# Two token columns to a list product: one-hots of 64 places, two of four blocks of the result in use

## The chip, the cores and the metric

One Trainium2 chip, one of its cores. The metric is the device time of one execution in microseconds (us). Engines are named as in the profile: PE is TensorE's matmul stream, PEld its weight loads, DVE is VectorE, ACT is ScalarE, POOL is GpSimd, SP is SyncE.

## The reference

A 2-D Fourier transform of `x`, a mixture of experts with a capacity for each expert, and a two-layer feed-forward network with a leaky activation:

```python
X = np.fft.fft(np.fft.fft(x, axis=1), axis=2).real          # x: 8 x 3072 x 256
x = X.reshape(24576, 256)

logits = x @ w_gate                                          # 8 experts
order = np.argsort(-logits.flatten())                        # best scores first
# each token goes to the first expert of this order that has room (cap = 3072 tokens)
for e in range(8):
    out[mask[e]] = np.maximum(x[mask[e]] @ w1[e], 0) @ w2[e]

h = out @ w_in
g = np.maximum(h, 0) + alpha * np.minimum(h, 0)
return g @ w_out
```

## The kernel before

It has two stages. The first (0 to about 370 us) does the Fourier transform and writes the tokens to DRAM, with their logits kept on the chip. The second (`ffn_phase`, the rest) fills the experts one after another, in eight rounds: a round finds the next expert to be full and its 3072 tokens, and the feed-forward network then runs over them in 6 tiles of 512 tokens, 48 tiles in all.

The network's products are split into high and low float32 parts, three matmuls for each. In the code of a tile (`for i in range(8)`) stand the layers `l1` (tile `h`), two of `l3` (tile `u`), `l2` (`y`) and two of `l4` (`o`), of the present and the previous tile: six steps to an `i`, each of 6 matmuls of 512 columns or 12 of 256. After a step's matmuls are written, one piece of the routing of the *next* expert is put in by `next(bg, None)`, and then the evacuation of that layer by ACT and DVE. The program is written out in this order and no scheduler moves it (`manual_schedule`): each engine works through its own instructions in the order in which they stand. `router.beat` counts the steps, and `yield from self.lag()` lets two of them go by, so that what DVE has just been given can be ready before TensorE comes to the matmul that reads it.

The last part of a round (`place`, then `pack`) makes the expert's token list. `si` is each token's place in the list (0 to 3071; others lie outside it). Tokens lie as 128 partitions x 192 columns. A place is split into a low part, `lh[:, 0]` (7 bits, 128 values), and a high part, `lh[:, 1]` (24 values in use). For each column of 128 tokens, a one-hot of the low part (`ol`, 128 wide) is the stationary operand, and a one-hot of the high part, multiplied once by the partition number (`self.pf`) and once by the column number (`self.colb`), is the moving operand (`rr`, 2 x 24 = 48 wide). The sum over all 192 columns, in the tile `ls`, is the list: for each place its token's partition and column. `pack` makes the one-hots for 8 columns at a time (a chunk: `eq`, `ol`, and two `rr` on DVE, lines 650 to 653), and after two chunks and a lag it issues their 16 matmuls (line 659). That is 12 groups of 16 to a list. The first list is made by another function (`pack_wide`); the other seven by `pack`, beside the network's matmuls. The list is then copied (`lm`), turned into row numbers (`idx`), and read by `gather_x`, which fetches the tokens of a tile by indirect DMAs from POOL's queue.

What loads the weights: each matmul reads one column of a chunk, `ol[:, :, j]`, that is 128 values that lie 8 elements apart.

Of the kernel before, what the change touches and what calls it, by code (L numbers as in the profile page):

```python
# [10 lines left out]
F32 = mybir.dt.float32  # L11
F32R = mybir.dt.float32r
BF16 = mybir.dt.bfloat16
I32 = mybir.dt.int32
I16 = mybir.dt.int16
# [3 lines left out]
ALU = mybir.AluOpType  # L19
# [4 lines left out]
P = 128  # L24
B, N, D = 8, 3072, 256
E = 8
TOK = B * N
N1, N2 = 96, 32
NG = 24
HC = 138  # L30
CV = 256
NCOL = TOK // P
# [236 lines left out]
class Router:  # L269
# [20 lines left out]
    def __init__(self, ctx, tc, LG):  # L290
        nc = self.nc = tc.nc
        self.LG = LG
        rp = ctx.enter_context(tc.tile_pool(name="r_state", bufs=1))
        V = nc.vector
        self.oh = rp.tile([P, NCOL, E], BF16, name="oh")
        self.aw = rp.tile([P, NCOL], BF16, name="aw")
        self.hi = rp.tile([P, NCOL], F32, name="hi")
        self.lo = rp.tile([P, NCOL], F32, name="lo")
        self.k16 = rp.tile([P, NCOL], I16, name="k16")
        self.done = rp.tile([P, NCOL], BF16, name="done")  # L300
        self.base = rp.tile([P, 1], F32, name="base")
        self.hstar = rp.tile([P, 1], F32, name="hstar")
        self.ohe = self.oh.rearrange("p a e -> p (a e)").rearrange("p (e a) -> p e a", e=E)
        self.eid = rp.tile([P, E], F32, name="eid")
        self.wm = rp.tile([P, 1], F32, name="wm")
        self.estar = rp.tile([P, 1], F32, name="estar")
        V.memset(self.done, 0.0)

        self.wE = rp.tile([P, E], BF16, name="wE")
        self.colb = rp.tile([P, NCOL], BF16, name="colb")  # L310
        self.mskj = rp.tile([P, 16], F32, name="mskj")
        self.mske = rp.tile([P, E], F32, name="mske")
        self.ones = rp.tile([P, P], F16, name="ones")
        self.onesb = rp.tile([P, NCOL], BF16, name="onesb")
        self.tri = rp.tile([P, P], BF16, name="tri")
        self.triA = rp.tile([96, NCOL], BF16, name="triA")
        self.triB = rp.tile([96, NCOL], BF16, name="triB")
        self.pf = rp.tile([P, 1], F32, name="pf")
        with tc.tile_pool(name="r_init", bufs=1) as ip:
            ci = ip.tile([P, NCOL], I32, name="ci")  # L320
            nc.gpsimd.iota(ci, pattern=[[1, NCOL]], base=0, channel_multiplier=0)
            cf = ip.tile([P, NCOL], F32, name="cf")
            V.tensor_copy(cf, ci)
            pi = ip.tile([P, 3], I32, name="pi")
            nc.gpsimd.iota(pi, pattern=[[0, 3]], base=0, channel_multiplier=1)
            V.tensor_copy(self.pf, pi[:, :1])
            V.tensor_scalar(self.wE, cf[:, :E], -1.0, float(E), op0=ALU.mult, op1=ALU.add)
            V.tensor_copy(self.colb, cf)
            V.tensor_copy(self.eid, cf[:, :E])
            V.tensor_scalar(pi[:, 1:2], pi[:, 0:1], 3, None, op0=ALU.logical_shift_right)  # L330
            V.tensor_scalar(pi[:, 2:3], pi[:, 0:1], 7, None, op0=ALU.bitwise_and)
            pq = ip.tile([P, 3], F32, name="pq")
            V.tensor_copy(pq, pi)
            V.tensor_scalar(self.mskj, cf[:, :16], pq[:, 1:2], None, op0=ALU.is_equal)
            V.tensor_scalar(self.mske, cf[:, :E], pq[:, 2:3], None, op0=ALU.is_equal)
            V.memset(self.ones, 1.0)
            V.memset(self.onesb, 1.0)

            V.tensor_scalar(self.tri, cf[:, :P], self.pf, None, op0=ALU.is_gt)
            V.tensor_scalar(self.triA, cf[:96], self.pf[:96], None, op0=ALU.is_gt)  # L340
            V.tensor_scalar(self.triB, cf[:96], self.pf[:96], 96.0, op0=ALU.subtract, op1=ALU.is_gt)

    def open_work(self, ctx, tc):
        self.wp = wp = ctx.enter_context(tc.tile_pool(name="r_work", bufs=1))
        self.ilo = wp.tile([P, P, self.CH], I16, name="ilo")
        self.ihi = wp.tile([P, self.CH, NG], I16, name="ihi")

    def prep(self, wp, view, n):
# [50 lines left out]
    def count_wide(self, psum, pool, key, lows, k, at0=None):  # L399
# [18 lines left out]
        for h, H in ((0, 10), (10, 10), (20, 4)):  # L418
            sh = [P, H, k - first, 8]
            V.tensor_tensor(  # L420
                ind[:, h : h + H, first:k], blocks(key)[:, h : h + H, None, :].broadcast_to(sh),
                lows[:, None, 16 - k + first :, :].broadcast_to(sh), op=ALU.is_ge,
            )
            for c in range(h, h + H):
                nc.tensor.matmul(
                    dv, ind[:, c, :k].rearrange("p k j -> p (k j)"), self.oh[:, 8 * c : 8 * c + 8],
                    start=(c == 0), stop=(c == NG - 1),
                )
# [15 lines left out]
    def first(self, psum, lists, pool):  # L444

        nc, wp = self.nc, self.wp
        V = nc.vector
# [6 lines left out]
            nc.gpsimd.iota(lows[step], pattern=[[step, 16], [0, 8]], base=-32768, channel_multiplier=0)  # L454
        ilo = pool.tile([P, P, 16], I16, name="ilo")
        nc.gpsimd.iota(ilo, pattern=[[1, P], [0, 16]], base=0, channel_multiplier=0)
        nc.gpsimd.iota(self.ilo, pattern=[[1, P], [0, self.CH]], base=0, channel_multiplier=0)
        nc.gpsimd.iota(self.ihi, pattern=[[0, self.CH], [1, NG]], base=0, channel_multiplier=0)
        yield "start"
        self.warm(24)  # L460
# [71 lines left out]
    def place(self, psum, lists, at, n, wide=None, ilo=None):  # L532


        nc, wp = self.nc, self.wp
        V = nc.vector
# [36 lines left out]
        si = wp.tile([P, NCOL], I16, tag="si", name="si")  # L573
        V.scalar_tensor_tensor(si, s12[:, 0], 30000.0, s12[:, 1], op0=ALU.add, op1=ALU.add)
        lh = wp.tile([P, 2, NCOL], I16, tag="lh", name="lh")
        V.tensor_scalar(lh[:, 0], si, 127, None, op0=ALU.bitwise_and)
        V.tensor_scalar(lh[:, 1], si, 7, None, op0=ALU.logical_shift_right)
        yield
        ls = psum(name="ls")
        lv = ls[:, : 2 * NG].rearrange("p (a g) -> p a g", a=2)  # L580
        lm, idx = lists
        yield from (self.pack_wide(wide, lv, lh, ilo) if wide else self.pack(lv, lh))
        V.tensor_copy(lm, lv)
        V.scalar_tensor_tensor(idx, lm[:, 1], float(P), lm[:, 0], op0=ALU.mult, op1=ALU.add)
        yield "list"
        if n == 1:
            return

        V.scalar_tensor_tensor(self.done, lh[:, 1], float(NG), self.done, op0=ALU.is_lt, op1=ALU.max)
        pen = wp.tile([P, 2, E - 1], F32, tag="pen", name="pen")  # L590
        for i, op in enumerate((ALU.is_le, ALU.is_gt)):
            V.tensor_scalar(pen[:, i, : n - 1], self.wE[:, : n - 1], self.wm, -BIG, op0=op, op1=ALU.mult)
# [2 lines left out]
        for c in range(-1, NCOL // H):  # L595
            g = self.LG[:, c * H : c * H + H] if c >= 0 else self.eid[:, None, :]
# [10 lines left out]
    def pack_wide(self, pool, lv, lh, ilo):  # L607

        nc, V = self.nc, self.nc.vector
        C = 16  # L610
        self.warm(14)
# [3 lines left out]
        H = NCOL // 4  # L615
        for c in range(0, NCOL, C):
            if c % H == 0:
# [10 lines left out]
                )  # L628
            ol = pool.tile([P, P, C], BF16, tag="ol", bufs=2, name="ol")
            V.tensor_tensor(ol, lh[:, 0, None, c : c + C].broadcast_to([P, P, C]), ilo, op=ALU.is_equal)  # L630
            for j in range(C):
                nc.tensor.matmul(
                    lv, ol[:, :, j], rr[:, c + j], start=(c + j == 0), stop=(c + j == NCOL - 1)
                )
            self.warm(2 if c % H == H - C else 1)
            yield

    def pack(self, lv, lh):

        nc, wp, V = self.nc, self.wp, self.nc.vector  # L640
        C = self.CH
        for c2 in range(0, NCOL // C, 2):
            made = []
            for c in (c2, c2 + 1):
                s = slice(c * C, c * C + C)
                ol = wp.tile([P, P, C], BF16, tag="ol", bufs=2, name="ol")

                eq = wp.tile([P, C, NG], BF16, tag="eq", bufs=2, name="eq")
                rr = wp.tile([P, C, 2, NG], BF16, tag="rr", bufs=2, name="rr")
                V.tensor_tensor(eq, lh[:, 1, s, None].broadcast_to([P, C, NG]), self.ihi, op=ALU.is_equal)  # L650
                V.tensor_tensor(ol, lh[:, 0, None, s].broadcast_to([P, P, C]), self.ilo, op=ALU.is_equal)
                V.tensor_scalar(rr[:, :, 0], eq, self.pf, None, op0=ALU.mult)
                V.tensor_tensor(rr[:, :, 1], eq, self.colb[:, s, None].broadcast_to([P, C, NG]), op=ALU.mult)
                made.append((c, ol, rr))
                yield
            yield from self.lag()
            for c, ol, rr in made:
                for j in range(C):
                    nc.tensor.matmul(  # L659
                        lv, ol[:, :, j], rr[:, j], start=(c == 0 and j == 0),  # L660
                        stop=(c == NCOL // C - 1 and j == C - 1),
                    )
            yield

    def rank(self, n):

# [691 lines left out]
```

## Time and profile before

| | |
|---|---|
| median of 3 runs | 3851.39 us (3847.69 to 3852.5) |
| profiled execution, its own time | 3852.32 us |
| its span, first to last instruction | 3850.2 us |
| granted TensorE clock, mean over the span | 0.994 of full |
| PE busy, share of the span | 3781.4 us, 98% |
| DVE busy | 2523.0 us, 66% |
| ACT busy | 1817.5 us, 47% |
| POOL busy | 566.2 us, 15% |

A share of busy time is an average over both stages. The ends of matmuls are modelled, and matmuls overlap, so what a matmul costs is read from the distance between starts, and not from its duration.

### The profile page before, as it was taken

What the parts mean: (1) busy time and instruction counts of PE and PEld (TensorE: products, weight loads), DVE (VectorE), ACT (ScalarE), POOL (GpSimd) and SP (SyncE); (2) the same over time, 40 slices, a digit from 0 to 9 for tenths busy, and PEclk for the clock granted to TensorE, in tenths of its full rate; (3) what the DMA queues carried; (4) which work ended last, traced back from release to release, by engine and by line L of the source; (5) the groups of instructions that cost most, each with busy time, mean ns of one, the idle gap of its engine ahead of it and who ended that gap; (6) DMA issues with size and microseconds to landing.
All of it is one profiled execution on the core that took longest, in us unless ns stands there. A gap on an engine that the chain in (4) does not pass through costs nothing.

```text
span 3850.2 us, 62081 instructions
## 1 busy us (share of the span) xinstructions
PE 3781.4 (98%) x23849; PEld 3334.9 (87%) x23859; DVE 2523.0 (66%) x7024; ACT 1817.5 (47%) x3455; POOL 566.2 (15%) x845
## 2 busy tenths in 40 slices
PE   8999799999999999999999999999999999999999
PEld 8998588887888888888888888888888888888888
DVE  5776765788768876787677776676544444444444
ACT  4554144444445554454454444444445545554444
POOL 2221210020001110020011110120111101111010
PEclk9999899999999999999999999999999999999999
DMA  8775200010000000010001000010001000000000
GB/s 230 203 214 176 78 17 12 7 42 15 12 12 28 28 22 13 12 45 12 12 23 31 15 23 12 16 41 12 12 23 34 23 12 23 28 20 20 12 17 12
DMA packets 95049, 153.51 MB, mean 40 GB/s; under 512 B 14688, under 2 KB 64544, under 8 KB 94752
## 3 DMA queue, kind: packets, MB, share of 16 engines
q0 software_dynamic: 30400, 90.21, 7.8%
q1 hardware_dynamic: 63440, 58.75, 5.5%
q8 instruction: 187, 3.06, 0.3%
q14 instruction: 110, 0.90, 0.1%
q10 hardware_dynamic: 912, 0.58, 0.1%
HBM read 90.77 MB, written 58.72 MB: 39 GB/s over the span
## 4 chain that ended last, share of the span: by engine, by line
PE 89%; DVE 4%; issue 3%; DMA 1%; ACT 1%; POOL 1%; another core or an unknown queue 0%; SPq 0%; POOLq 0%; ACTq 0%
PE o L1123 26%; PE u L1043 25%; PE y L1043 13%; PE h L1043 13%; PE b L209 4%; PE a L150 2%; PE ls L659 2%; PE c L226 2%; DVE junk L857 2%; PE xps L1033 1%; DMA x<-in_x 1%; DVE g L1101 1%; DVE r L1096 1%; ACT a L1095 0%
## 5 line engine op out<-in xcount | busy, mean ns | idle before, releaser
L1123 PEld LDWEIGHTS o<-w3t,g 128*128 128x128 f32 x9216 | 1133.1, 188 | 43.7 <-DVE g L1101 8.2
L1123 PE MATMUL o<-w3t,g 128*128 128x256 f32 x9216 | 1153.2, 280 | 8.0 <-DVE g L1101 5.9
L1043 PE MATMUL u<-ys,w3t 128*128 128x512 f32 x4608 | 1122.5, 391 | 0.4 <-issue 0.2
L1043 PEld LDWEIGHTS u<-ys,w3t 128*128 128x128 f32 x4608 | 859.7, 188 | 176.9 <-DVE ys L1079 0.8
L1096 DVE SCALAR_TENSOR_TENSOR r<-a,nal,r 128x512 f32<-128x512 f32 x768 | 576.5, 751 | 638.0 <-ACT a L1095 606.2
L1094 ACT ACTIVATE r<-u 128x512 f32<-128x512 f32 x768 | 459.8, 599 | 736.4 <-DVE g L1101 316.7
L1056 ACT ACTIVATE hs<-h 128x512 fp32r<-128x512 f32 x384 | 230.4, 600 | 838.6 <-PE h L1043 799.1
L1146 POOL DMA_INDIRECT out_dram<-os,orow x192 | 191.4, 997 | 2622.5 <-ACT os L1142 2555.0
L1057 DVE SCALAR_TENSOR_TENSOR hs<-h,hs 128x512 fp32r<-128x512 f32 x384 | 264.8, 690 | 409.0 <-ACT hs L1056 406.9
L1101 DVE TENSOR_TENSOR g<-r,g 128x512 fp32r<-128x512 f32 x768 | 525.9, 685 | 4.1
L1043 PE MATMUL y<-hs,wxh 128*128 128x512 f32 x1536 | 491.7, 401 | 7.9 <-ACT hs L1056 7.9
L1100 ACT CAST g<-r 128x512 fp32r<-128x512 f32 x768 | 477.0, 621 | 17.2 <-DVE r L1096 16.6
L1095 ACT ACTIVATE a<-u 128x512 f32<-128x512 f32 x768 | 455.0, 592 | 0.0
L1043 PEld LDWEIGHTS y<-hs,wxh 128*128 128x128 f32 x1536 | 283.8, 189 | 67.9 <-ACT hs L1056 8.4
L1043 PE MATMUL h<-xth,wxh 128*128 128x512 f32 x768 | 304.4, 396 | 0.4 <-DVE hs L1057 0.3
L1043 PE MATMUL y<-hs,wxl 128*128 128x512 f32 x768 | 304.1, 396 | 0.0
L1043 PE MATMUL h<-xtl,wxh 128*128 128x512 f32 x768 | 301.3, 392 | 0.2 <-issue 0.2
L1043 PE MATMUL h<-xth,wxl 128*128 128x512 f32 x768 | 300.0, 391 | 0.0
L857 DVE TENSOR_SCALAR_CACHE_REDUCE junk<-ke 128x192 bf16<-128x192 uint16 x960 | 276.5, 347 | 0.1
L1017 POOL DMA_INDIRECT xg<-XD,idx x192 | 207.9, 1083 | 102.7 <-issue 55.8
L1043 PEld LDWEIGHTS y<-hs,wxl 128*128 128x128 f32 x768 | 144.5, 188 | 35.2
L1043 PEld LDWEIGHTS h<-xth,wxl 128*128 128x128 f32 x768 | 144.6, 188 | 32.4
(257 smaller groups left out, 3571.6 us busy)
## 6 DMA issues: line engine op xcount, KB each, us to landing
x<-in_x SPq DMA_DIRECT2D x63, 384.0 KB, 4.7
XD<-xs SPq DMA_DIRECT2D x96, 128.0 KB, 2.9
XD<-xs SPq DMA_DIRECT2D x184, 64.0 KB, 2.8
raw<-in_w POOLq DMA_DIRECT2D x32, 256.0 KB
W3S<-hl POOLq DMA_DIRECT2D x32, 256.0 KB
w3t<-W3S SPq DMA_DIRECT2D x16, 512.0 KB, 9.8
tw<-in_tw POOLq DMA_DIRECT2D x12, 512.0 KB
xg<-XD,idx POOLq DMA_INDIRECT x192
```

What stands on the lines that cost most here:

```text
L857: V.tensor_scalar(junk[(e + k) % 2], ke[:, e], float((k + 1) * step), 0.0, op0=ALU.is_ge, op1=ALU.add, accum_out=s[:, e, k : k + 1],)
L1017: nc.gpsimd.indirect_dma_start(out=x[:, j, :], out_offset=None, in_=XD, in_offset=bass.IndirectOffsetOnAxis(ap=idx[:, j0 + j : j0 + j + 1] ...
L1043: nc.tensor.matmul(o, w, a, start=(first and n == 0), stop=(last and n == 2))
L1056: nc.scalar.activation(h[:, 0], ps, AF.Relu)
L1057: nc.vector.scalar_tensor_tensor(h[:, 1], ps, 0.0, h[:, 0].bitcast(F32), op0=ALU.max, op1=ALU.subtract)
L1094: nc.scalar.activation(r, ps, AF.Relu)
L1095: nc.scalar.activation(a, ps, AF.Relu, scale=-1.0)
L1096: nc.vector.scalar_tensor_tensor(r, a, nal[:, j : j + 1], r, op0=ALU.mult, op1=ALU.add)
L1100: nc.scalar.copy(g[:, 0], r)
L1101: nc.vector.tensor_sub(g[:, 1], r, g[:, 0].bitcast(F32))
L1123: nc.tensor.matmul(o[:, s, :], a, w, start=(j == 0 and n == 0 and s % 2 == 0), stop=(j == 15 and n == 2 and s % 2 == 1), skip_group_check= ...
L1146: ins = nc.gpsimd.indirect_dma_start(out=out, out_offset=bass.IndirectOffsetOnAxis(ap=orow[:, jj : jj + 1], axis=0), in_=os[:, s, :], in_o ...
```

## The change

Two token columns go into one matmul. The low part of a place now has 6 bits (64 values) and the high part 48 values. The stationary operand is the one-hots of two columns, 2 x 64 = 128 wide, interleaved (`j :: 4`, elements 4 apart); the moving operand is both columns' `rr`, 2 x 2 x 48 = 192 wide. The result has four blocks, column against column; the two in which a column meets itself are of use, the other two are masked out by `self.odd` (partition parity). Four small products with `self.unpair`, a shifted identity made once at the start, add the two useful blocks and bring the list back to its old form of 128 x 48, in a new tile `lv`. A group has 8 matmuls in the place of 16, and there are still 12 groups to a list. `pack_wide` is not touched: its list still splits at 7 bits.

```diff
@@ open_work, first
-        self.ilo = wp.tile([P, P, self.CH], I16, name="ilo")
+        self.ilo = wp.tile([P, 64, self.CH], I16, name="ilo")
+        self.ih2 = wp.tile([P, 2 * NG], I16, name="ih2")
...
-        nc.gpsimd.iota(self.ilo, pattern=[[1, P], [0, self.CH]], base=0, channel_multiplier=0)
+        nc.gpsimd.iota(self.ilo, pattern=[[1, 64], [0, self.CH]], base=0, channel_multiplier=0)
+        nc.gpsimd.iota(self.ih2, pattern=[[1, 2 * NG]], base=0, channel_multiplier=0)
@@ __init__: once, at the start
+            hp = ip.tile([P, 2], I32, name="hp")
+            V.tensor_scalar(hp[:, :1], pi[:, :1], 1, None, op0=ALU.logical_shift_right)
+            V.tensor_scalar(hp[:, 1:], pi[:, :1], 1, None, op0=ALU.bitwise_and)
+            hf = ip.tile([P, 2], F32, name="hf")
+            V.tensor_copy(hf, hp)
+            V.tensor_scalar(self.unpair, cf, -64.0, hf[:, :1], op0=ALU.add, op1=ALU.is_equal)
+            V.tensor_copy(self.odd[:, 1:], hf[:, 1:])
+            V.tensor_scalar(self.odd[:, :1], hf[:, 1:], -1.0, 1.0, op0=ALU.mult, op1=ALU.add)
@@ place
-        V.tensor_scalar(lh[:, 0], si, 127, None, op0=ALU.bitwise_and)
-        V.tensor_scalar(lh[:, 1], si, 7, None, op0=ALU.logical_shift_right)
-        yield
-        ls = psum(name="ls")
-        lv = ls[:, : 2 * NG].rearrange("p (a g) -> p a g", a=2)
+        w = 7 if wide else 6
+        V.tensor_scalar(lh[:, 0], si, (1 << w) - 1, None, op0=ALU.bitwise_and)
+        V.tensor_scalar(lh[:, 1], si, w, None, op0=ALU.logical_shift_right)
+        yield
@@ pack
-    def pack(self, lv, lh):
+    def pack(self, psum, lh):
+        C, G = self.CH, 2 * NG
+        ps = psum(name="ls")[:, : 4 * G]
...
-                ol = wp.tile([P, P, C], BF16, tag="ol", bufs=2, name="ol")
-                eq = wp.tile([P, C, NG], BF16, tag="eq", bufs=2, name="eq")
-                rr = wp.tile([P, C, 2, NG], BF16, tag="rr", bufs=2, name="rr")
-                V.tensor_tensor(eq, lh[:, 1, s, None].broadcast_to([P, C, NG]), self.ihi, op=ALU.is_equal)
-                V.tensor_tensor(ol, lh[:, 0, None, s].broadcast_to([P, P, C]), self.ilo, op=ALU.is_equal)
+                ol = wp.tile([P, 64, C], BF16, tag="ol", bufs=2, name="ol")
+                rr = wp.tile([P, C, 2, G], BF16, tag="rr", bufs=2, name="rr")
+                eq = rr[:, :, 1]
+                V.tensor_tensor(
+                    eq, lh[:, 1, s, None].broadcast_to([P, C, G]), self.ih2[:, None, :].broadcast_to([P, C, G]),
+                    op=ALU.is_equal,
+                )
+                V.tensor_tensor(ol, lh[:, 0, None, s].broadcast_to([P, 64, C]), self.ilo, op=ALU.is_equal)
                 V.tensor_scalar(rr[:, :, 0], eq, self.pf, None, op0=ALU.mult)
-                V.tensor_tensor(rr[:, :, 1], eq, self.colb[:, s, None].broadcast_to([P, C, NG]), op=ALU.mult)
+                V.tensor_tensor(eq, eq, self.colb[:, s, None].broadcast_to([P, C, G]), op=ALU.mult)
...
-                for j in range(C):
+                for j in range(C // 2):
                     nc.tensor.matmul(
-                        lv, ol[:, :, j], rr[:, j], start=(c == 0 and j == 0),
-                        stop=(c == NCOL // C - 1 and j == C - 1),
+                        ps.rearrange("p (c k) -> p c k", c=2), ol.rearrange("p l c -> p (l c)")[:, j :: C // 2],
+                        rr[:, j :: C // 2].rearrange("p c v g -> p c (v g)"),
+                        start=(c + j == 0), stop=(c == NCOL // C - 1 and j == C // 2 - 1),
                     )
             yield
+        both = wp.tile([P, 2, 2, NG, 2], BF16, tag="ae", name="both")
+        for c in range(2):
+            V.tensor_scalar(
+                both[:, c].rearrange("p v g h -> p (v g h)"), ps[:, c * 2 * G : (c + 1) * 2 * G],
+                self.odd[:, c : c + 1], None, op0=ALU.mult,
+            )
+        yield from self.lag()
+        lv = psum(name="lv")[:, : 2 * NG].rearrange("p (a g) -> p a g", a=2)
+        for h in range(2):
+            for c in range(2):
+                nc.tensor.matmul(
+                    lv, self.unpair[:, 64 - 64 * h : 192 - 64 * h], both[:, c, :, :, h], start=(h + c == 0), stop=(h + c == 2)
+                )
+        yield
+        return lv
```

TensorE, the eleventh group of the list of round 1 in the kernel before (`h` and `u` are the network's layers, `ls` the list's sum): the rows up to the group's first weight load and matmul. Sixteen such pairs stand there, and then the other 6 matmuls of a `u`.

```order
L1043 MATMUL h_7_9369<-xth_8607,wxh_5169 128x512
L1043 MATMUL h_7_9369<-xtl_8608,wxh_5169 128x512
L1043 MATMUL h_7_9369<-xth_8607,wxl_5177 128x512
L1043 MATMUL u_14_9379<-ys_8629,w3t_5160 128x512 x6
L659 LDWEIGHTS ol
L659 MATMUL ls<-rr,ol 128x48
```

The same place in the changed kernel:

```order
L1080 MATMUL h_7_9279<-xth_8597,wxh_5180 128x512
L1080 MATMUL h_7_9279<-xtl_8598,wxh_5180 128x512
L1080 MATMUL h_7_9279<-xth_8597,wxl_5188 128x512
L1080 MATMUL u_14_9289<-ys_8619,w3t_5171 128x512 x6
L680 LDWEIGHTS ol
L680 MATMUL ls<-rr,ol 128x192
```

The group stands after the same layer; it now has 8 pairs, and a matmul of it has 192 columns in the place of 48.

DVE, one chunk of the same list in the kernel before, between the evacuations of the layers (`g`, `hs`); the second chunk of the pair follows it with the same four rows:

```order
L1101 TENSOR_TENSOR g_12_8457<-r_12_8421,g_12_8457 128x512
L650 TENSOR_TENSOR eq<-lh,ihi 128x192
L651 TENSOR_TENSOR ol<-lh,ilo 128x1024
L652 TENSOR_SCALAR rr<-eq,pf 128x8x24
L653 TENSOR_TENSOR rr<-eq,colb 128x8x24
```

And in the changed kernel (`ih_5125` is the tile `ih2`):

```order
L1138 TENSOR_TENSOR g_12_8459<-r_12_8431,g_12_8459 128x512
L668 TENSOR_TENSOR rr<-lh,ih_5125 128x8x48
L672 TENSOR_TENSOR ol<-lh,ilo 128x512
L673 TENSOR_SCALAR rr<-rr,pf 128x8x48
L674 TENSOR_TENSOR rr<-rr,colb 128x8x48
```

The four rows stand where they stood; three of them work on twice the elements, and `ol` on half.

TensorE in the changed kernel, after that list's last group: the matmuls that bring the list back, behind a layer `h` of the following tile. Four such pairs stand there; the kernel before has nothing in this place.

```order
L1080 MATMUL h_1_9489<-xth_9372,wxh_5174 128x512
L1080 MATMUL h_1_9489<-xtl_9373,wxh_5174 128x512
L1080 MATMUL h_1_9489<-xth_9372,wxl_5182 128x512
L696 LDWEIGHTS unpair
L696 MATMUL lv<-both,unpair 128x48
```

These are added, two layers after the last group, as `lag` has it; the copy to `lm` follows one layer later.

## Rows read from the trace of the kernel before

**Rows 1.** The page, chain that ended last, shares by engine.

```profile
PE 89%; DVE 4%; issue 3%; DMA 1%; ACT 1%; POOL 1%; another core or an unknown queue 0%; SPq 0%; POOLq 0%; ACTq 0%
```

**Rows 2.** Waits of PE, 448 to 3850 us: total, times, longest (us).

```profile
PE cnt L848 <- DVE junk L857: 12.8, 15, 2.5
...
PE o L1123 <- DVE g L1101: 5.9, 9, 1.4
...
PE ls L659 <- DVE rr L653: 0.2, 1, 0.2
```

**Rows 3.** Groups by line: the list's matmuls.

```profile
L659 PE MATMUL ls<-rr,ol 128*128 128x48 bf16 x1344 | 97.9, 220 | 0.2 <-DVE rr L653 0.2
```

**Rows 4.** Chain in order of time, 1800 to 1830 us: start, us, what.

```profile
1810.27 0.22 PE tot L543 x4
...
1811.94 2.81 PE o L1123 x24
1814.75 0.68 PE pos L565 x8
...
1816.85 2.74 PE u L1043 x12
...
1825.16 1.00 PE ls L659 x16
1826.17 2.84 PE u L1043 x12
```

**Rows 5.** Timeline of PE around one list group: start, us.

```profile
688.45 1.53 PE L1043 MATMUL u<-ys,w3t 128*128 128x512 f32 x6
689.83 1.17 PE L659 MATMUL ls<-rr,ol 128*128 128x48 bf16 x16
690.84 1.64 PE L1043 MATMUL u<-ys,w3t 128*128 128x512 f32 x6
692.31 0.40 PE L1043 MATMUL y<-hs,wxh 128*128 128x512 f32 x1
```

**Rows 6.** Timeline of PE around the 8 matmuls of line 565, 192 columns each.

```profile
669.98 1.53 PE L1043 MATMUL u<-ys,w3t 128*128 128x512 f32 x6
671.35 0.26 PE L565 MATMUL pos<-at,tri 128*128 128x192 bf16 x1
...
671.97 1.64 PE L1043 MATMUL u<-ys,w3t 128*128 128x512 f32 x6
673.45 0.40 PE L1043 MATMUL y<-hs,wxh 128*128 128x512 f32 x1
```

**Rows 7.** Groups by line, DVE: the chunk's operations and wider ones.

```profile
L651 DVE TENSOR_TENSOR ol<-lh,ilo 128x1024 bf16<-128x1024 int16 x168 | 115.1, 685 | 5.4 <-PE ls L659 5.4
...
L650 DVE TENSOR_TENSOR eq<-lh,ihi 128x192 bf16<-128x192 int16 x168 | 59.0, 351 | 0.1
...
L652 DVE TENSOR_SCALAR rr<-eq,pf 128x192 bf16<-128x192 bf16 x168 | 44.5, 265 | 0.0
...
L630 DVE TENSOR_TENSOR ol<-lh,ilo 128x2048 bf16<-128x2048 int16 x12 | 14.3, 1221 | 0.6 <-PE ls L632 0.5
...
L620 DVE TENSOR_TENSOR eq<-lh,ihi 128x1152 bf16<-128x1152 int16 x4 | 5.4, 1352 | 0.0
```

**Rows 8.** Timeline: a pair's last DVE operation, and its group on PE.

```profile
679.63 0.35 DVE L653 TENSOR_TENSOR rr<-eq,colb 128x192 bf16<-128x192 bf16 x1
...
681.78 0.80 PE L659 MATMUL ls<-rr,ol 128*128 128x48 bf16 x10
```

**Rows 9.** Busy time by engine in the stretch of one list (PE, PEld, DVE, ACT, POOL).

```profile
1059.00:1154.00 95.00, 94.77 (x672) 83.50 (x671) 66.00 (x144) 40.83 (x75) 8.91 (x12) 1.00 0.04 12
```

**Rows 10.** Timeline: the list of round 1 ready, and the first gather from it.

```profile
781.83 0.18 DVE L584 SCALAR_TENSOR_TENSOR idx<-lm 128x24 int32<-128x24 f32 x1
...
826.43 1.03 POOL L1017 DMA_INDIRECT xg<-XD,idx  x1 [0.30 <-PE u L1043]
```

More of the change, by code (lines that the diff above doesn't have):

```diff
@@ L318, in __init__ @@
         self.pf = rp.tile([P, 1], F32, name="pf")
+        self.unpair = rp.tile([P, NCOL], BF16, name="unpair")
+        self.odd = rp.tile([P, 2], F32, name="odd")
         with tc.tile_pool(name="r_init", bufs=1) as ip:
@@ L575, in place @@
         lh = wp.tile([P, 2, NCOL], I16, tag="lh", name="lh")
-        V.tensor_scalar(lh[:, 0], si, 127, None, op0=ALU.bitwise_and)
-        V.tensor_scalar(lh[:, 1], si, 7, None, op0=ALU.logical_shift_right)
+        w = 7 if wide else 6
+        V.tensor_scalar(lh[:, 0], si, (1 << w) - 1, None, op0=ALU.bitwise_and)
+        V.tensor_scalar(lh[:, 1], si, w, None, op0=ALU.logical_shift_right)
         yield
-        ls = psum(name="ls")
-        lv = ls[:, : 2 * NG].rearrange("p (a g) -> p a g", a=2)
         lm, idx = lists
-        yield from (self.pack_wide(wide, lv, lh, ilo) if wide else self.pack(lv, lh))
+        if wide:
+            lv = psum(name="ls")[:, : 2 * NG].rearrange("p (a g) -> p a g", a=2)
+            yield from self.pack_wide(wide, lv, lh, ilo)
+        else:
+            lv = yield from self.pack(psum, lh)
         V.tensor_copy(lm, lv)
@@ L587, in place @@
             return
-        V.scalar_tensor_tensor(self.done, lh[:, 1], float(NG), self.done, op0=ALU.is_lt, op1=ALU.max)
+        V.scalar_tensor_tensor(self.done, lh[:, 1], float(TOK // E >> w), self.done, op0=ALU.is_lt, op1=ALU.max)
         pen = wp.tile([P, 2, E - 1], F32, tag="pen", name="pen")
@@ L636, in pack_wide @@
             yield
-    def pack(self, lv, lh):
+    def pack(self, psum, lh):
         nc, wp, V = self.nc, self.wp, self.nc.vector
-        C = self.CH
+        C, G = self.CH, 2 * NG
+        ps = psum(name="ls")[:, : 4 * G]
         for c2 in range(0, NCOL // C, 2):
```

## The prediction

> **What bounds the kernel now.** First the chain that ended last: 89% of it is PE [rows 1]. Then the waits of PE over the whole network stage, 448 to 3850 us: the longest total is 12.8 us for the search's counts, then 5.9 us for DVE's `g` [rows 2]. In 3400 us that is nothing: the stage lasts as long as its matmuls follow each other. So a matmul group that takes less of PE's time shortens the kernel by the same amount, as long as nothing else becomes late. The list's groups lie in this stage: 1344 matmuls of 48 columns, 84 groups of 16, seven lists of 12 [rows 3].
>
> Since PE's durations overlap, I read costs from starts. The chain in order of time gives them: 12 matmuls of 512 columns take 2.74 us (0.228 each), 24 of 256 columns 2.81 us (0.117 each), 8 of 192 columns 0.68 us (0.085 each), and a list group's 16 of 48 columns 1.00 us (0.0625 each) [rows 4]. From 512 to 256 columns the step falls by 0.111 us, that is 0.43 ns a column, and only 0.006 us is left over that does not depend on the columns. At that rate 48 columns would stream in 0.021 us; the group takes 0.0625. Something other than columns sets its step; as each of these matmuls has its own weights, I take it to be the weight load, whose time is then at most 0.0625 us. This is the reason to expect a gain: columns are added where the step isn't set by columns.
>
> **The change, part by part.** *The group on PE.* 192 columns at 0.43 ns are 0.083 us, and with the fixed part 0.089; the row of line 565, with exactly this shape (192 bf16 columns, 128 weights wide), has 0.085 [rows 4]. That is more than the 0.0625 of the load, so the load should be hidden behind the matmul before it. It is hidden in the wide float32 layers, by the 0.006 us. I take 0.68 us for the new group, against 1.00 us: a gain of 0.32. A second reading takes the tail too. From the six `u` ahead to the `y` behind, a list group's surroundings take 692.31 - 688.45 = 3.86 us [rows 5], and the same surroundings with line 565's eight matmuls 673.45 - 669.98 = 3.47 us [rows 6]; without anything between, twelve `u` are 2.74 [rows 4]. Net that is 1.12 against 0.73, a gain of 0.39. The difference between the readings is the tail: behind a list group twelve `u` take 2.84 us and not 2.74 [rows 4], and this need not stay as long. But line 565 reads its weights from neighbouring elements, the new group from every fourth, so I don't take the whole of it: 0.35 us a group, bounds 0.32 and 0.39. Times 84: **-29.4 us**, bounds -26.9 and -32.8.
>
> *The four products with `unpair`.* The nearest row is line 543, four matmuls of 128 columns with weights of neighbouring elements: 0.22 us [rows 4]. The upper bound is a quarter of a list group's net, 0.28 us; nothing is the lower. Seven lists: **+1.5 us**, bounds 0 and 2.0. Two steps (some 2.8 us, two times six matmuls of 0.228) lie between `both` and these matmuls, so PE should not wait for DVE here. `lv` takes the buffer of `ls` (the pool has one), and needs `both` to have been read from it; that is the same wait.
>
> *DVE.* The operation of `eq` costs 351 ns at 192 elements and 1352 at 1152, so 1.04 ns an element; `ol` 685 ns at 1024 and 1221 at 2048, 0.52 ns an element [rows 7]. Per chunk: `eq` +0.20 us; the second `rr` has the same form, +0.20; `ol` -0.27; the first `rr` (265 ns now) between nothing and the 0.20 of `eq`, I take +0.10. Sum +0.23 us, bounds 0.13 and 0.33; for 168 chunks 39 us more of DVE. On the path this costs nothing if DVE has room: in the stretch of one list it is busy 66.0 of 95 us [rows 9]. 24 chunks add 5.5, and the stretch loses 12 x 0.35 = 4.2: 71.5 of 90.8, 79%. The latest reader is the group's first matmul: the pair's last DVE operation ends at 679.63 + 0.35 = 679.98, and PE comes to the group at 681.78, 1.8 us later [rows 8]. Two chunks take 0.46 (at most 0.66) of this, and PE, now 0.35 earlier, up to as much again: 0.8 us at the least are left there. Over all groups PE has waited 0.2 us for line 653 [rows 2]. I put **+0.5 us** for cases in which DVE is busier, bounds 0 and 7 (0.08 a group). `both` adds 14 operations of 96 columns, each less than the 0.35 of `eq`, under 5 us and in the same cover.
>
> *What is later.* The list is ready some four steps later (two of lag, one for `both`, one behind the products), about 5.6 us, less what the 12 groups save. Behind it wait `lm`, `idx` and then POOL's gathers. In round 1, the earliest, `idx` ends at 782 us and POOL comes to the gather at 826 [rows 10]: 44 us of cover. Without it, the gather and with it the next tile would move one for one.
>
> *The rest.* Six small DVE operations at the start, before DVE has its first evacuation to make; one iota on POOL halved and a small one added. Nothing on the path.
>
> Sum against the profiled execution: 3852.3 - 29.4 + 1.5 + 0.5 = 3824.9. Its time lies 0.9 us above the median of the runs (3851.4), so **3824 us** for the median, 0.7% faster; with all bounds on one side 3818 to 3835.
>
> **The rivals.** *1. The load is not hidden, so nothing is gained.* The weights lie 4 elements apart, and no row has such weights ahead of a long matmul. If load and columns followed one another, today's 0.0625 would be 0.021 of columns and 0.042 of load; then the new step is 0.083 + 0.042 = 0.125, eight are 1.00 us, the gain is nothing, and the products leave it at 3853. If the load alone takes the 0.0625, the step is 0.146, a group 1.17, and the time 3851.4 + 84 x 0.17 + 1.5 = 3867. Against it: the wide layers, whose step has only 0.006 us besides its columns. A rule speaks for it. The Trainium skill (TensorE: Matmul & The Clock Gate, The mechanism, under Part 3) says that a weight load overlaps matmuls in flight only when it goes to another row group, and both operands here take all the rows; the trace disagrees with it as far as the wide layers go, with that 0.006 us.
>
> *2. The load is hidden, but is the longer of the two.* If a load with this pattern took about 0.105 us, between the 192-column step and the 0.125 above, the group would be 0.84 us, a gain of 0.16 x 84 = 13 us, 3840. Against it: today's load, whose elements lie still further apart, fits in 0.0625. The Trainium skill (same page, LDWEIGHTS (loading the stationary operand)) puts 128 columns at 128 / 1.2 = 107 ns, by which this case would be the right one; the trace has 62.5 ns for a whole step, so it disagrees.
>
> *3. PE waits for DVE; slower.* DVE's pair of chunks grows by 0.46 us, and PE is there sooner. If PE waits on the average more than 27.4 / 84 = 0.33 us a group at `rr`, or at `g` and `hs` behind it, the gain is gone, and beyond that the kernel is slower: at 0.6 us a group 3824 + 50 = 3874. For it: DVE's work comes in bursts, and `g` is late at times already, 9 times, 1.4 us at worst [rows 2]. Against it: the 79%, and the 1.8 us.
>
> *4. The later list shifts the search.* The next round's search waits at places set by where its steps fall, 12.8 us in all [rows 2]. A shift could move some of it either way, by some us; it stays inside the range, unless a list comes too late for its tile, against which stand the 44 us.
>
> **How the numbers follow.** The forecast has 0.82, rival 2 (or a partly hidden load) 0.06, rival 1 0.05 (0.03 no change, 0.02 slower), rival 3 0.05 (0.02 no change, 0.03 slower), rival 4 with a late list 0.02 (one half each for no change and slower). A measurement of this kernel tells a change of 0.2%, 7.7 us, from none. So faster 0.88, same 0.06, slower 0.06. The range: the bounds of the forecast alone are 3818 to 3835; I extend the upper end a little towards rival 2, to 3838, which leaves out rivals 1 and 3.
>
> **What would show it.** In the changed kernel: a group of 8 with 0.66 to 0.72 us from its first start to the next layer; pairs of groups inside one tile 0.35 us closer; 672 matmuls of 192 columns; PE's waits for `rr` under 2 us in all; `eq` and the second `rr` near 0.55 us, `ol` near 0.42, the first `rr` 0.27 to 0.47; DVE about 40 us busier in all; the four `unpair` matmuls 0.1 to 0.3 us; the gather of round 1 without a wait for `idx`. The prediction is wrong if the step of the new matmuls is over 0.1 us, or if waits of PE for DVE grow by more than 5 us.

## The result, and the profile of the changed kernel

The changed kernel takes 3815.39 us (median of 6 runs, 3813.86 to 3818.08). The kernel before has 3848.0 us over six runs; the three that the prediction started from have a median of 3851.39, three new ones 3846.56. The ratio is 0.9916 (95% interval [0.9905, 0.9928]), that is 32.6 us less, 0.85% faster. The forecast was 3824 us, the range 3818 to 3838: the direction is right, and the time lies 2.6 us under the range.

The page of the changed kernel, profiled at 3817.1 us: the span, the busy time of each engine with its share and number of instructions, and the chain that ended last.

```profile
span 3814.7 us, 60835 instructions
...
PE 3752.8 (98%) x23205; PEld 3305.2 (87%) x23215; DVE 2571.3 (67%) x7044; ACT 1815.2 (48%) x3455; POOL 560.8 (15%) x846
...
PE 89%; DVE 4%; issue 3%; DMA 1%; ACT 1%; POOL 0%; another core or an unknown queue 0%; SPq 0%; POOLq 0%; ACTq 0%
```

The chain has the same shares as before but for POOL's, which was 1% [rows 1]. PE stays the bound, and the span fell by 35.5 us. DVE is busy 48.3 us more (2523.0 before).

The groups by line: after the bar the busy time in us, the mean of one in ns, and the idle time just before them with what ended it.

```profile
L680 PE MATMUL ls<-rr,ol 128*128 128x192 bf16 x672 | 71.8, 250 | 0.1
...
L680 PEld LDWEIGHTS <-ol 128*128 128x128 bf16 x672 | 54.0, 116 | 18.0 <-issue 12.3 <-DVE g L1138 2.8 <-DVE hs L1094 1.6
...
L696 PE MATMUL lv<-both,unpair 128*128 128x48 bf16 x28 | 1.9, 186 | 0.0
```

There are 672 matmuls in the place of 1344 [rows 3], and no wait for `rr` is named; a load's record is 116 ns, where it had 165 with weights 8 apart. What a group takes of PE is read from starts. First the chain in order of time (start, length, what), around one group of a later round, which answers to [rows 4]:

```profile
1823.18 2.72 PE u L1080 x12
1825.90 0.69 PE ls L680 x8
1826.59 1.42 PE y L1080 x6
```

And PE's timeline (start, us) at the place of [rows 5]:

```profile
687.29 1.53 PE L1080 MATMUL u<-ys,w3t 128*128 128x512 f32 x6
688.66 0.85 PE L680 MATMUL ls<-rr,ol 128*128 128x192 bf16 x8
689.30 1.63 PE L1080 MATMUL u<-ys,w3t 128*128 128x512 f32 x6
690.77 0.62 PE L1080 MATMUL y<-hs,wxh 128*128 128x512 f32 x2
```

From the first `u` to the `y` it is 690.77 - 687.29 = 3.48 us, against 3.86 before [rows 5] and 3.47 around line 565 [rows 6]. This group gained 0.38 us: by starts it takes 689.30 - 688.66 = 0.64 us where it took 1.01, and the six `u` behind take 1.47 in both. Over all 84 groups the time from a group's first start to the next layer adds up to 84.9 us before and 53.7 after: **-31.2 us**, 0.37 a group. Inside a group the median steps were 87, 64, then 60 to 62 ns; now they are 111, six of 82 or 83, and 28 ns to the next layer.

DVE at the second chunk of a list's first pair (start, us), and PE's group behind it; the rows of lines 674 and 680 answer to [rows 8].

```profile
678.09 0.55 DVE L668 TENSOR_TENSOR rr<-lh,ih 128x384 bf16<-128x384 int16 x1
678.56 0.42 DVE L672 TENSOR_TENSOR ol<-lh,ilo 128x512 bf16<-128x512 int16 x1
678.89 0.31 DVE L673 TENSOR_SCALAR rr<-rr,pf 128x384 bf16<-128x384 bf16 x1
679.24 0.56 DVE L674 TENSOR_TENSOR rr<-rr,colb 128x384 bf16<-128x384 bf16 x1
679.71 0.68 DVE L1094 SCALAR_TENSOR_TENSOR hs<-h,hs 128x512 fp32r<-128x512 f32 x1
...
680.98 0.85 PE L680 MATMUL ls<-rr,ol 128*128 128x192 bf16 x8
```

From `eq`'s start to that of the operation behind the chunk it is 679.71 - 678.09 = 1.62 us; by medians 1.63, and 1.32 before. The chunk grew by 0.31 us (forecast 0.23, bounds 0.13 and 0.33). This pair ends at 679.80, and PE comes 1.2 us later. Over the 84 groups the median is 1.29 us (1.58 before), but 23 pairs end less than 0.67 us ahead of their group's first start (5 before), and 5 end after it; a group reads the second chunk from its fifth matmul on, 0.36 us later. In the stretch of a list DVE is busy 74.45 of 95 us (66.00 before [rows 9]; the row has PE, PEld, DVE, ACT, POOL, as there):

```profile
1053.60:1148.60 95.00, 95.00 (x606) 83.24 (x605) 74.45 (x148) 42.89 (x80) 12.71 (x18) 1.00 0.05 15
```

The products with `unpair`, the list of round 1 ready, and the gather (start, us; compare [rows 10]):

```profile
780.28 0.27 PE L696 MATMUL lv<-both,unpair 128*128 128x48 bf16 x4
780.40 3.00 PE L1080 MATMUL u<-ys,w3t 128*128 128x512 f32 x12
783.24 0.63 PE L1080 MATMUL y<-hs,wxh 128*128 128x512 f32 x2
...
782.40 0.18 DVE L601 SCALAR_TENSOR_TENSOR idx<-lm 128x24 int32<-128x24 f32 x1
...
819.66 1.31 POOL L1054 DMA_INDIRECT xg<-XD,idx  x1 [0.30 <-PE y L1080]
```

The products take 780.40 - 780.28 = 0.12 us up to the next layer's first start, and the layer behind them takes longer: twelve `u` have 783.24 - 780.40 = 2.84 us here, 2.72 in the chain above. Its first step is the long one (0.31 to 0.32 us where a step of 512 columns is 0.23); behind a list group it is as long in both kernels and drops out of their difference, but here nothing stood before. By the starts from the last matmul ahead to the seventh behind, against the same layers with nothing between, the products cost 0.19 to 0.24 us a list, 1.4 us for seven. The gather comes 37 us after the list; the wait shown at it is for a layer, as before, and not for `idx`.

Last, PE's waits from 448 to 3850 us (total, times, longest), beside [rows 2]:

```profile
PE cnt L885 <- DVE junk L894: 8.6, 11, 2.4
PE y L1080 <- ACT hs L1093: 7.8, 1, 7.8
PE o L1160 <- DVE g L1138: 3.7, 7, 0.7
PE o L1160 <- DVE r L1133: 2.0, 2, 1.3
```

The 7.8 us for `hs` is one wait where the kernel before has one of 7.9, which the prediction passed over in its list. The waits for `g` didn't grow (5.9 before), 2.0 us for `r` are new, and the waits for the counts fell from 12.8 to 8.6 us. The last was not in the sum: the groups and the products together give -29.8 us, and the network stage, from tile 1's first transposes to the end, lost 34.6 (3369.5 to 3334.9). Two questions were open: why the step of the old group was 61 ns, and what the moved search is worth.

### The profile page after: what moved, and what is told of

Read it like the earlier page. It is cut to its first block, busy times and chain, and to the rows that moved or that the text cites. A ratio compares the mean times of both kernels' runs of the same rounds, so it can differ in the third digit from the quotient of the medians.

```text
span 3814.7 us, 60835 instructions
## 1 busy us (share of the span) xinstructions
PE 3752.8 (98%) x23205; PEld 3305.2 (87%) x23215; DVE 2571.3 (67%) x7044; ACT 1815.2 (48%) x3455; POOL 560.8 (15%) x846
## 4 chain that ended last, share of the span: by engine, by line
PE 89%; DVE 4%; issue 3%; DMA 1%; ACT 1%; POOL 0%; another core or an unknown queue 0%; SPq 0%; POOLq 0%; ACTq 0%
PE o L1160 26%; PE u L1080 25%; PE y L1080 13%; PE h L1080 13%; PE b L209 4%; PE a L150 3%; PE c L226 2%; DVE junk L894 2%; PE ls L680 1%; PE xps L1070 1%; DMA x<-in_x 1%; DVE r L1133 1%; DVE g L1138 1%; DMA XD<-xs 0%
## 5 line engine op out<-in xcount | busy, mean ns | idle before, releaser
L1080 PEld LDWEIGHTS y<-hs,wxl 128*128 128x128 f32 x768 | 144.7, 188 | 35.2
```

The source lines that it names most:

```text
L1080: nc.tensor.matmul(o, w, a, start=(first and n == 0), stop=(last and n == 2))
```

## The experiments

These runs were made on three chips, with the kernel before beside them on each: the layouts without packing and the three added steps on one, the changed kernel again and its variants on another (there too the second look at the two-apart layout), the rest on a third. The kernel before takes 3835.9 to 3837.6 us on them, so each kernel is read by its ratio to it. "Step" is the distance between matmul starts in a group, "group sum" the 84 groups as above.

**Distance between weights, without any packing.** The kernel before, with the one-hot tile laid out so that a matmul's 128 weights lie 4, 2 or 1 elements apart (8 before). For 2; the other two have 4 and 1 in its place:

```diff
-ol = wp.tile([P, P, C], BF16, tag="ol", bufs=2, name="ol")
+ol = wp.tile([P, C // 2, P, 2], BF16, tag="ol", bufs=2, name="ol")
-V.tensor_tensor(ol, lh[:, 0, None, s].broadcast_to([P, P, C]), self.ilo, op=ALU.is_equal)
+lo = lh[:, 0, s].rearrange("p (a b) -> p a b", b=2).unsqueeze(2).broadcast_to([P, C // 2, P, 2])
+V.tensor_tensor(ol, lo, self.ilo, op=ALU.is_equal)
-lv, ol[:, :, j], rr[:, j], ...
+lv, ol[:, j // 2, :, j % 2], rr[:, j], ...
```

(`ilo` and its iota take the same layout.)

> The kernel before, with 16 matmuls of 48 columns to a group as ever, but the one-hots of a chunk laid out so that a column's 128 weights lie 4 elements apart and not 8. Theory A (the step of 0.0625 us is the weight load, and the load is slow because of the distance between weights): the record of a load was 167 ns at a distance of 8, 113 ns at 4 in the changed kernel and 96 ns for neighbouring weights with a step of 0.025, so the step should fall to about 0.034, the group from 1.00 to about 0.55 us, and the time by 84 x 0.45 = 38 us, to about 3810: as fast as the change or faster, without packing two columns. Theory B (a matmul with its own weights costs 0.0625 whatever the distance, and only fewer matmuls help): step and time as before, 3848.

> As s4, with a distance of 2 elements. Theory A: step 0.025 to 0.034, group 0.42 to 0.55 us, 3800 to 3810; DVE's ol keeps its 685 ns if runs of 2 elements are enough for its rate of two a cycle, and takes about 1.2 us if not. Theory B: 3848.

> As s4, with neighbouring weights (distance 1), for which DVE reads the same token value 128 times in a row. Theory A: step 0.025, group 0.42 us, 84 x 0.58 = 49 us less, 3800, if DVE's ol, which I expect to fall to one element a cycle (1.15 us in the place of 0.69, 0.9 us more a pair), stays covered. Theory B: 3848 or slower.

Measured: 4 apart 0.9911 [0.9898, 0.9925]; 2 apart 0.9876 [0.9861, 0.9891], 47.9 us faster; adjacent 0.9903 [0.9888, 0.9918]. The chain shows a group of each, first 4 apart:

```profile
1826.73 0.56 PE ls L660 x16
```

2 apart:

```profile
1828.00 0.42 PE ls L660 x16
```

Adjacent:

```profile
1817.14 0.41 PE ls L660 x16
```

The step is 33, 25 and 25 ns, where 8 apart has 61 [rows 4: 1.00 us for 16]. The columns at 0.43 ns and the 6 ns beside them give 27 ns for 48. So the prediction was right that the load sets the step, and the load's time comes from the distance between weights; at 2 and at 1 element the step is no longer than this estimate for the columns alone, so nothing of the load is seen in it. The group sums are 46.7, 35.2 and 41.2 us. Why the adjacent layout gains less than that of 2, its rows by line show:

```profile
L652 DVE TENSOR_TENSOR ol<-lh,ilo 128x1024 bf16<-128x1024 int16 x168 | 205.1, 1221 | 0.0
...
L660 PE MATMUL ls<-rr,ol 128*128 128x48 bf16 x1344 | 49.9, 184 | 4.5 <-DVE rr L654 4.5
```

And those of 2 apart:

```profile
L652 DVE TENSOR_TENSOR ol<-lh,ilo 128x1024 bf16<-128x1024 int16 x168 | 115.4, 687 | 4.1 <-PE ls L660 4.1
...
L660 PE MATMUL ls<-rr,ol 128*128 128x48 bf16 x1344 | 48.4, 184 | 0.0
```

With one token's value repeated along the whole inner axis, DVE makes `ol` in 1221 ns; with runs of two values it keeps 687, as before [rows 7], and PE doesn't wait. The adjacent layout is 9.4 us slower than two apart; 6.0 of these lie in the groups (4.5 are named as waits for `rr`), and the rest is not located. Two apart, with no pairing at all, beats the changed kernel by some 13 us by the ratios. Pairing doubles the columns streamed, 16 x 48 to 8 x 192; here it paid only against the slow load.

**Adjacent weights in the changed kernel.**

```diff
-ol = wp.tile([P, 64, C], BF16, tag="ol", bufs=2, name="ol")
+ol = wp.tile([P, C // 2, 64, 2], BF16, tag="ol", bufs=2, name="ol")
-ol.rearrange("p l c -> p (l c)")[:, j :: C // 2], rr[:, j :: C // 2]...
+ol[:, j].rearrange("p l c -> p (l c)"), rr[:, 2 * j : 2 * j + 2]...
```

> The changed kernel with the pair of columns laid out side by side, so that a matmul's 128 weights are neighbours. Theory (the load is hidden behind 192 columns at a distance of 4 already): a step stays at 0.082 to 0.083 us; only the first step of a group, 0.111, may fall to 0.085, 84 x 0.026 = 2 us. If the load still costs something in the changed kernel, the step falls below 0.082 and the gain is larger.

Measured: 0.9907 [0.9892, 0.9922], not told apart from the changed kernel on the same chip (`again`, below). Its chain:

```profile
1821.85 0.68 PE ls L681 x8
```

The steps stay at 82 and 83 ns; only the first falls, from 111 to 93, and the group sum goes from 53.7 to 52.1. The load 4 apart was hidden in the changed kernel; columns set its step.

**The added steps alone.** Before the list is ready, the change adds three steps (two of `lag`, one behind the products). Here they are added to the kernel before, with no other change; then six of them.

```diff
@@ pack, behind its loop
+        yield from self.lag()
+        yield
```

> The kernel before with three more steps between the last group of a list and its copy, as the change has them for its small products, and nothing else. It tests what moved the search's waits (12.8 us before, 8.6 after). If the shift of the next round's search by some steps does it: about 4 us faster, 3844, and the waits of the counts near 8.6 us. If the shorter groups do it, or if it varies from run to run: 3848, and waits of 12 to 13 us.

> The kernel before with six more steps behind a list, where three gave 6.5 us. If starting the search later is what helps: 6 us or more. If it is only at which layers its counts fall (a step later by six is one whole round of the layers, so they meet the same layers again as with none): about nothing, and the waits of the counts near 12 us again.

Measured: three steps 0.9983 [0.9974, 0.9992], 6.5 us faster (3.1 to 10.0), with the groups as before (84.6 us); six steps 0.9995 [0.9986, 1.0004], nothing. PE's waits from 785 to 1030 us, the search of round 2, in the kernel before (the profile at the end of this section):

```profile
PE cnt L848 <- DVE junk L857: 10.4, 12, 1.7
PE o L1123 <- DVE g L1101: 4.0, 6, 1.1
```

With three steps:

```profile
PE cnt L850 <- DVE junk L859: 7.1, 10, 1.7
PE o L1125 <- DVE g L1103: 4.3, 6, 1.3
```

With six:

```profile
PE cnt L851 <- DVE junk L860: 7.7, 13, 1.7
PE o L1126 <- DVE g L1104: 3.4, 5, 0.7
PE h L1046 <- DVE hs L1060: 1.3, 1, 1.3
```

The search comes to other layers of the network, and PE waits less for its counts. Three steps made the network stage 5.3 us shorter in the trace, in tiles 5 to 8 (counted from 0; over the others the differences cancel); the waits named explain 3.5 of them (14.9 to 11.4 us in all in this stretch), and the rest is not located. With six, these waits fall by 2.3 us and the stage by 3.9 in the trace, and in time nothing can be told: more steps are not better, and how far the waits go by place is only partly explained.

**The changed kernel again, and with its search moved back.** In the second, three steps of the bookkeeping that `place` does behind the list are dropped, so that the next round's search stands at the same layers as in the kernel before; the list itself stays three steps late.

```diff
@@ place, the loop that moves the bookkeeping
-            yield
+            if wide or c not in (1, 3, 5):
+                yield
```

> The changed kernel, unchanged, beside the other kernels of this call, so that they are compared on one chip. Its groups give 84.9 - 53.7 = 31.2 us by the traces; with the shift of the search's waits (6.5 us, as the run with three more steps and nothing else measured) and less some 0.7 us for the small products, 37 us below the kernel before, ratio 0.9904. If the shift is worth nothing here: 30.5 us, 0.992.

> The changed kernel with the next round's search back at the network steps at which the kernel before has it: behind a list of pack, three steps of the following bookkeeping are put together with their neighbours, so that the three added steps are made up for. Theory (part of the gain is the search's waits, moved by those three steps): 4 to 7 us slower than the changed kernel, waits of the counts back near 12 us, ratio near 0.992 to before. Rival (the waits fall because the groups are shorter, or at random): as the changed kernel.

Measured: 0.9909 [0.9894, 0.9924] again, and 0.9936 [0.9922, 0.9949] moved back, 11.8 us slower. The same waits, of the changed kernel:

```profile
PE cnt L885 <- DVE junk L894: 7.1, 10, 1.7
PE o L1160 <- DVE g L1138: 4.3, 6, 1.4
```

Moved back:

```profile
PE cnt L886 <- DVE junk L895: 10.3, 12, 1.7
PE o L1161 <- DVE g L1139: 5.7, 7, 1.4
```

The counts' waits have the values of `shift` in the changed kernel, and those of the kernel before when the search is moved back. But the edit does more than that: DVE has the bookkeeping's operations in fewer steps, and over the whole network stage PE waits 8.0 us for `g` and not 5.1. So 11.8 is more than the shift is worth, and some 3 us of it are not located. The run shows the sign and the place; the size is that of `shift`.

**DVE's cover.** The changed kernel makes `ol` twice: 0.335 us more for each chunk, 56 us in all, and no other work.

```diff
 V.tensor_tensor(ol, lh[:, 0, None, s].broadcast_to([P, 64, C]), self.ilo, op=ALU.is_equal)
+V.tensor_tensor(ol, lh[:, 0, None, s].broadcast_to([P, 64, C]), self.ilo, op=ALU.is_equal)
```

> The changed kernel with ol made twice in each chunk: 168 x 0.335 = 56 us more work for DVE in the stretches of the lists, 0.67 us for each pair of chunks, and nothing else. If DVE's work is covered there, as the prediction has it: up to 2 us slower than the changed kernel. If DVE is at its limit already (the rival in which PE waits for rr): some 0.3 to 0.67 us a group, 25 to 56 us slower.

Measured: 0.9966 [0.9954, 0.9978], by the ratios some 22 us slower than the changed kernel, 0.26 us a group: just under the second expectation. The group sum, 53.7 there, is 71.4. Its waits of PE from 448 to 3850 us:

```profile
PE ls L681 <- DVE rr L675: 14.8, 17, 2.1
PE cnt L886 <- DVE junk L895: 7.3, 11, 1.7
PE o L1161 <- DVE g L1139: 5.3, 9, 1.3
```

In a list's stretch DVE is busy 79.49 of 95 us:

```profile
681.00:776.00 95.00, 93.53 (x590) 81.57 (x590) 79.49 (x165) 44.09 (x81) 11.49 (x18) 1.00 0.07 20
```

At 84% busy, PE already waits 17 times, up to 2.1 us. The changed kernel is at 78% and no wait for `rr` is named in it (by starts, one group's fifth matmul comes 0.23 us late). So 0.67 us more a pair is more than the cover that is left in some groups, as the 23 pairs above would have it, while the median pair still has room.

**The two gains together.** The two-apart kernel, and the same with three steps (the diffs of both above).

> The kernel before with weights 2 elements apart once more, for one look beside the others of this call: group 0.42 us, and some 10 us below the changed kernel.

> Both things that helped, without the packing of two columns: weights 2 elements apart, 16 matmuls of 48 columns to a group, and three more steps behind each list. If the two gains add up: the one run gave 47.9 us, the other 6.5, so 54 us below the kernel before, ratio 0.986, and some 17 us faster than the changed kernel. If the shift is worth nothing beside shorter groups: 0.9876, as without it.

The first is the two-apart kernel without added steps, a second look at it: 3791.72 us in one run, 8.6 below the changed kernel beside it, the group again 0.420 us. With the three steps: 0.9871 [0.9856, 0.9886], the lowest of all (median 3786.14 us), but the interval holds both 0.986 and 0.9876, so the time doesn't tell whether the gains add up. In the traces, of two chips, its network stage is 6.2 us shorter (3315.2 to 3309.0), and the counts' waits over the whole stage, 11.6 us without the steps, are

```profile
PE cnt L851 <- DVE junk L860: 7.3, 11, 1.7
```

**The kernel before, with another profile.**

> The kernel before, unchanged, for its trace on the chip of this call: waits of the counts in the round-2 search at the same counts and of the same lengths as in its first trace (12.8 us in all), if they are set by the order of the program and not by chance.

It took 3837.33 us in one run. Its round-2 search waits at the same counts as in the first trace, all but one with the same length within 0.1 us (11.4 us in the whole stage, 12.8 there), so the places are set by the order of the program. Its network stage is 3365.2 us, that of the changed kernel in its second profile, on another chip, 3330.1: 35.1 us less. The groups are 30.8 of it (84.5 to 53.7), the three steps alone 5.3 by their trace, and the products take back 1.4; these add up to 34.7.

## Why the prediction missed its range

**What failed.** Rival 4: "A shift could move some of it either way, by some us; it stays inside the range". I saw that the steps move the search and left it out of the sum, at nothing. Alone it is worth 6.5 us (3.1 to 10.0), as much as the 6 us between forecast and low end; in the traces of the result, the counts' waits fell by 4.2 us, and the 34.6 us of the stage are 4.8 more than groups and products give. It also should have widened the low end, since its sign was open: the range was made of the groups' and DVE's bounds only. That it came out as a gain was luck; six steps gave nothing. I also counted four steps where three were added. Neither sign that I had named for being wrong came up (steps over 0.1 us, waits for DVE up by 5 us): the miss lies in a term that they didn't cover.

**Mis-sized.** The groups gave 31.2 us (30.8 by the second pair of profiles), not 29.4: 0.37 us each. Of my two readings, 0.39 was the nearer. I put their difference on a tail behind the group, but that was a misreading: six `u` behind take 692.31 - 690.84 = 1.47 us in [rows 5] and 673.45 - 671.97 = 1.48 in [rows 6]. The chain has 0.68 us for line 565's eight matmuls, where their starts give 671.97 - 671.35 = 0.62; the new group has 0.64. Weights 4 apart cost something only in the first step, 111 ns against 93 for adjacent ones. The products took 1.4 us, near the 1.5 of the sum, and the waits for DVE nothing and not 0.5; together the three terms are 2.4 us. The bounds, added up from 3851.4, are 3818.6 and 3833.5, where I wrote 3818 and 3835.

**The base.** The median of before moved from 3851.4 to 3848.0 as runs were added. These 3.4 us are more than the 2.6 by which the time lies under the range, but they are no error of the mechanism: as a ratio the forecast was 0.9929, just outside the measured [0.9905, 0.9928], and the low end was 0.9913, just under the measured 0.9916. It took both, the lower base and the shift, to leave the range.

**What held.** PE's starts bound the stage. The load set the step of the 48-column matmuls, as their starts shrank with the distance alone (61, 33, 25 ns) at the same columns. The new load is hidden behind 192 columns: 82 to 83 ns a step against the forecast 83 to 89. So rivals 1 and 2 are out, since each needs 105 ns or more. Rival 3 is out for this change: no wait for `rr` is named, and the waits for `g` stood at 3.7 us, and at 5.1 in the changed kernel's second profile (4.8 in that of the kernel before); the 2.0 us for `r` did not come again there. Yet its point of decision was nearer than "DVE has room" made it sound. The chunk grew by 0.31 us, and 0.67 us more a pair costs 0.26 us of each group, some 70% of what the change gained there. I leaned on the mean share of the stretch and on one group with 1.8 us, and took 0.8 us as the least that is left; 5 pairs of the changed kernel end after their group has begun.

**What the prediction did not ask.** It took the load's 61 ns as given. They came from the layout of `ol`, and a change of the layout takes them away with no second matmul stage and no more work for DVE.

## What to carry to other kernels

Where the starts of matmuls lie further apart than their columns take, look at how far apart the elements of the stationary operand lie before the product is rebuilt: try a layout that brings them within two elements while the engine that writes the tile keeps its rate. Price what a change does to the place of background work that the bound engine waits for, by a run that adds the empty steps alone, and let the range take both signs until then. Read a cover from the tightest pair and not from one, or from a mean share (78% was enough here, 84% was not), and test it by adding to the work it hides. Count what added matmuls cost up to a few matmuls behind them: half of it can lie in the next layer.

## What the runs showed of the hardware

- A load of 128 bf16 weights paced matmuls of 48 columns by the distance of its elements: a step of 61 ns at 8 elements and 33 at 4; at 2 and at 1 it was 25, where 48 columns alone would take an estimated 27, by the rate from [rows 4]. Behind 192 columns the load was hidden at 4 elements: a step of 82 to 83 ns there and with adjacent weights. The first step of a group falls likewise: 87, 56 and 40 ns at 8, 4 and 2.
- DVE kept 687 ns for the 1024 elements of `ol` when a value was repeated only outside runs of two; repeated along the inner axis, it took 1221 ns.
- A layer of 512 columns behind a group of bf16 matmuls started with a long step, 0.31 to 0.32 us where its steps are 0.23, whether the group had 16 x 48, 8 x 192 or 4 x 48 columns.
